# Chunked attention and a two-layer network on one core: the same work written in a new order

## The chip, the core and the metric

The kernel runs on one core of a Trainium2 chip. The metric is the time of one execution in microseconds (us) on the device, lower is better. The figure for the kernel before is the median of three runs.

## The reference

The inputs are q, k and v of 4 batches, 8 heads, 768 positions and 64 dimensions, 8 memory rows of keys and values for each batch and head, and the network's weights. Attention is computed in 24 chunks of 32 positions; each chunk sees the memory rows and its neighbourhood of 16 positions to the left and 8 to the right. The result, 3072 tokens of 512 numbers, goes through a two-layer network.

```python
scores = scale * np.matmul(q_c, k_full.transpose(0, 1, 3, 2))
a = np.exp(scores - max); a = a / sum
out[:, :, c_start:c_end] = np.matmul(a, v_full)
...
x = attn_out.transpose(0, 2, 1, 3).reshape(B * S, H * D)
h = x @ w_in                                   # 512 -> 2048
g = h + np.sin(alpha * h) ** 2 / (alpha + 1e-09)
return g @ w_out                               # 2048 -> 512
```

## The kernel before, in words

The order of all work is written out by hand as lists of two- to five-letter words, one list for a front and one for each of four passes (lines 813 to 841). `Stage.run` takes them one by one and calls the function `do_` plus the first letter; what follows is the argument. Each engine executes its own instructions in the order in which the words issue them; semaphores between engines follow from the tiles that the instructions read and write.

The front (`Stage(-1)`) computes the attention of batch 0. Pass i (0 to 3) computes the network of batch i and, in between, the attention of batch i+1, so that pass 3 has only the network.

The words that the change and the prediction speak of:

- `aNE` casts the f32 piece N of batch 0's keys (0 to 3) or queries (4 to 7) to bf16 on engine E (line 650; V is DVE, A is ACT, P is POOL). The eight pieces `kq_f` are loaded at the start by the SP queue, in the order key 0, query 0, key 1, query 1 and so on (lines 712 to 720).
- `kN`, `lN` transpose a piece on TensorE (line 269), `KNE`, `LNE` copy it out of PSUM on engine E (lines 282 and 297).
- `Vbhh` loads the values of heads h to h of batch b by two or three DMAs of the POOL queue (line 160); `dm` loads the memory values of all batches; `mN` and `H` put them among the values (lines 187 and 193).
- `IxY` loads columns of w_in, 128 for each hexadecimal digit from x up to y, in one DMA of the POOL queue (line 212); `Uxy` loads rows of w_out in the same way; `dq108` and `dk108` load all queries and keys of batch 1; `R` issues the row loads of batches 2 and 3. So `I02` brings the weights of hidden tiles 0 and 1, `I27` those of tiles 2 to 6, and `I7g` those of tiles 7 to 15.
- `s` are the scores of attention blocks with their exponentials on ACT (lines 314 and 376), `v` is the product with the values, normed on DVE (lines 339, 350 and 403), `t` (DVE) and `T` (ACT) transpose the result on TensorE and copy it into the network's input `xT` (line 362), and `c` transposes by DMA.
- `bN` and `hN` are the two halves of hidden tile N of the first layer: four matmuls each of 384 columns (line 418). `hN` also issues the sine on ACT (line 435). `qNE` squares it on engine E (line 441) and `gN` combines it into `gT` on DVE, which frees the tile's two PSUM banks (line 449). There are eight banks, hence four hidden tiles in flight.
- `fN` issues the next N matmuls of the second layer, each of 512 columns (lines 32 and 457). Where a row of output is complete, `close` copies it out on DVE or ACT and stores it by the SP queue (line 465).
- `zN` issues N matmuls on zeros, which compute nothing; `W` and `e` load an activation table and say which engines do the copies of `close`.

In the front's list the transposed attention result must be complete for the first half of the columns before `b0`, and for the second half before `h0`. In pass 0, hidden tile 7 is the eighth tile; it is the first one that needs `I7g`.

The POOL engine issues its DMAs itself, in order with its own arithmetic. At most eight of its DMAs are outstanding at a time: the DMA semaphores are taken in turn, so that the ninth waits until the first one has landed.

Of the kernel before, what the change touches and what calls it, by code (L numbers as in the profile page):

```python
# [15 lines left out]
F32 = mybir.dt.float32  # L16
ACTF = mybir.ActivationFunctionType
ALU = mybir.AluOpType


class Feed:
# [64 lines left out]
def kernel(  # L86
# [263 lines left out]
    def normed(otv, bs):  # L350
# [5 lines left out]
            in1=rinv[:].unsqueeze(3).to_broadcast([QW, 2, HP, D]),  # L356
            op=ALU.mult,
        )
# [82 lines left out]
    def squared(t, eng):  # L441
# [3 lines left out]
        else:  # L445
            e = nc.vector if eng == "V" else nc.gpsimd
            e.tensor_tensor(out=s2[:], in0=u[:], in1=u[:], op=ALU.mult)  # L447

    def finish(t, gT):
# [3 lines left out]
            in0=t["s2"][:], scalar=inv_alpha[:, ft:ft + 1], in1=t["hT"][:, :, 0:HALF],  # L453
            op0=ALU.mult, op1=ALU.add,
        )
# [275 lines left out]
    def const_b():  # L731
        for col, lo, hi in rows:
            nc.vector.tensor_reduce(
                out=biasm[:, col:col + 1], in_=ident[:, lo:hi], op=ALU.add, axis=mybir.AxisListType.X
            )
        for col in (0, 3):
            nc.vector.tensor_tensor(
                out=biasm[:, col:col + 1], in0=biasm[:, col:col + 1], in1=biasm[:, 5:6], op=ALU.add
            )
        nc.vector.tensor_scalar(  # L740
            out=biasm[:, 0:5], in0=biasm[:, 0:5], scalar1=-NEG, scalar2=NEG,
            op0=ALU.mult, op1=ALU.add
        )
# [59 lines left out]
    def const_s():  # L803
# [6 lines left out]
    first = {}  # L810
    stage = Stage(-1, None)
    stage.tile = first
    stage.run((
# [3 lines left out]
    ))  # L817
    for i, words in enumerate(((
# [6 lines left out]
    ),(  # L825
# [5 lines left out]
    ),(  # L831
# [5 lines left out]
    ),(  # L837
# [3 lines left out]
    ))):  # L841
        stage = Stage(i, stage.nx).run(words)
    feed.take(400)

# [28 lines left out]
```

## Time and profile before

| | |
|---|---|
| median of three runs | 216.53 us (216.51, 216.53, 219.29) |
| span of the profiled execution, first to last instruction | 213.1 us |
| median less span | 3.4 us |
| TensorE (PE) busy | 201.7 us, 95% of the span |
| DVE, ACT, POOL busy | 66%, 67%, 47% |
| packets of the POOL's DMA queue (q0) | 92.3% of 16 engines' span |

The profile shows one execution. Busy times are shares of the span, the chain of waits goes back from the last instruction to what released it at each step, and the table of DMA issues gives the time from issue to landing. The profiled execution's own time on the device is its span of 213.1 us and what lies around it; of the three runs, the median is 3.4 us above that span.

### The profile page before, as it was taken

The page shows a single profiled execution, that of the slowest core. Times are in us where ns is not written, and L with a number is a line of the kernel's source. Part 1 is how long each engine was busy: PE and PEld are TensorE (multiplying, and loading weights), DVE is VectorE, ACT ScalarE, POOL GpSimd, SP SyncE. Part 2 cuts the span into 40 slices and gives each one's busy share as a digit, 9 for nine tenths or more (in the row PEclk, how much of TensorE's full clock was granted, in tenths as well). Part 3 has the DMA queues.
Part 4 walks back from the last instruction along what each step waited for, and adds up shares of the span by engine and source line. Part 5 has one row for each costly group of instructions (what it writes and reads, how often), then busy time and mean ns, then how long its engine had stood idle before and what let it go on. Part 6 is the DMA issues. An engine that isn't in the chain of part 4 may idle for free.

```text
span 213.1 us, 4479 instructions
## 1 busy us (share of the span) xinstructions
PE 201.7 (95%) x1721; PEld 113.5 (53%) x1721; DVE 140.5 (66%) x218; ACT 143.5 (67%) x230; POOL 99.8 (47%) x140
## 2 busy tenths in 40 slices
PE   0799899999999999999999999999999999999994
PEld 0456555565455556555455555554555555554443
DVE  7598678999542749975856649898157197865011
ACT  2597898976857469977846199887846289891110
POOL 8959515688598193009991039659400023200000
PEclk9999999999999999999999999999999999999999
DMA  6999999999999999969999229989945400000312
GB/s 195 337 163 141 193 209 205 204 163 182 131 177 141 137 148 144 180 88 110 126 217 171 72 63 131 156 126 129 175 115 123 124 15 0 2 3 0 148 49 98
DMA packets 95908, 28.19 MB, mean 132 GB/s; under 512 B 84864, under 2 KB 92432, under 8 KB 95888
## 3 DMA queue, kind: packets, MB, share of 16 engines
q0 software_dynamic: 68736, 13.25, 92.3%
q1 hardware_dynamic: 26976, 14.62, 28.2%
q8 instruction: 13, 0.21, 0.4%
q14 instruction: 7, 0.06, 0.1%
q10 hardware_dynamic: 176, 0.04, 0.1%
HBM read 29.66 MB, written 6.29 MB: 169 GB/s over the span
## 4 chain that ended last, share of the span: by engine, by line
PE 71%; DVE 9%; DMA 7%; ACT 4%; issue 4%; POOL 3%; DVEq 0%; POOLq 0%; ACTq 0%
PE ps L462 38%; PE ps L424 27%; DMA memv_st<-in_mem_v_dram 4%; DVE gT L451 4%; DVE s L447 3%; DMA vw<-in_v_dram 3%; PE ps L414 3%; PE ps L385 2%; ACT u L439 2%; PE ps L366 1%; ACT s L444 1%; POOL s L447 1%; POOL vw L172 1%; DVE kT L285 1%; ACT L699 1%
## 5 line engine op out<-in xcount | busy, mean ns | idle before, releaser
L462 PE MATMUL ps<-w_out_sb,gT 128*128 128x512 bf16 (+2 forms) x400 | 89.1, 371 | 0.0
L424 PE MATMUL ps<-xT,w_in_sb 128*128 128x384 bf16 x512 | 86.0, 326 | 0.7 <-DVE gT L451 0.4
L451 DVE SCALAR_TENSOR_TENSOR gT<-s,inv_alpha,ps 128x768 bf16<-128x768 f32 x64 | 63.0, 1011 | 12.5 <-ACT s L444 5.2
L424 PEld LDWEIGHTS <-w_in_sb 128*128 128x128 bf16 x512 | 49.8, 98 | 35.4 <-issue 2.1
L439 ACT ACTIVATE u<-ps,alpha_sb 128x768 f32<-128x768 f32 x64 | 56.6, 895 | 16.8 <-PE ps L424 14.3
L462 PEld LDWEIGHTS <-gT 128*128 128x128 bf16 x400 | 36.6, 98 | 37.9 <-DVE gT L451 0.2
L447 POOL TENSOR_TENSOR s<-u 128x768 f32<-128x768 f32 x11 | 17.4, 1582 | 69.7 <-ACT u L439 69.7
L399 ACT ACTIVATE pt<-ps,biasm 128x256 bf16<-128x256 f32 x72 | 27.2, 489 | 10.5 <-PE ps L385 10.5
L469 DVE COPY o_sb<-ps 128x512 f32<-128x512 f32 (+1 forms) x15 | 10.1, 678 | 28.3 <-PE ps L462 26.4
L447 DVE TENSOR_TENSOR s<-u 128x768 f32<-128x768 f32 x23 | 21.9, 953 | 7.8 <-ACT u L439 7.8
L444 ACT ACTIVATE s<-u 128x768 f32<-128x768 f32 x30 | 25.0, 841 | 0.5
L354 DVE TENSOR_TENSOR x_blk<-ps,rinv 96x512 bf16<-96x512 f32 x32 | 22.0, 687 | 1.1
L469 ACT COPY o_sb<-ps 128x512 f32<-128x512 f32 (+1 forms) x10 | 5.6, 562 | 21.6 <-PE ps L462 21.6
L172 POOL DMA_DIRECT2D vw<-in_v_dram x13 | 12.9, 994 | 7.9 <-PE ps L366 5.4
L353 DVE RECIPROCAL rinv<-ps 96x8 f32<-96x8 f32 x32 | 6.4, 200 | 13.5 <-PE ps L414 12.7
L179 POOL DMA_DIRECT2D vw<-in_v_dram x13 | 12.7, 976 | 0.0
L238 POOL DMA_DIRECT2D kst<-in_k_dram x16 | 12.2, 760 | 1.1 <-DMA vw<-in_v_dram 0.8
L232 POOL DMA_DIRECT2D kst<-in_k_dram x16 | 11.3, 708 | 2.3 <-DMA vw<-in_v_dram 1.6
L369 ACT COPY xT<-ps 128x384 bf16<-128x384 bf16 x12 | 5.6, 496 | 8.2 <-PE ps L366 8.2
L245 POOL DMA_DIRECT2D q_bf<-in_q_dram x12 | 10.7, 912 | 0.0
L414 PEld LDWEIGHTS <-pt 128*128 128x128 bf16 x192 | 8.2, 97 | 4.2 <-ACT pt L399 0.3
L414 PE MATMUL ps<-vw,pt 128*128 128x65 bf16 x192 | 8.9, 193 | 0.0
(81 smaller groups left out, 131.4 us busy)
## 6 DMA issues: line engine op xcount, KB each, us to landing
out_dram<-o_sb SPq DMA_DIRECT2D x23, 256.0 KB, 2.3
kq_f<-in_k_dram SPq DMA_DIRECT2D x4, 384.0 KB, 6.5
kq_f<-in_q_dram SPq DMA_DIRECT2D x4, 384.0 KB, 6.0
q_bf<-in_q_dram POOLq DMA_DIRECT2D x12, 128.0 KB, 6.7
w_in_sb<-in_moe_w_in_dram POOLq DMA_DIRECT2D x1, 1152.0 KB, 12.6
vw<-in_v_dram POOLq DMA_DIRECT2D x7, 128.0 KB, 6.7
vw<-in_v_dram POOLq DMA_DIRECT2D x8, 112.0 KB, 7.4
kst<-in_k_dram POOLq DMA_DIRECT2D x14, 64.0 KB, 5.1
```

The lines of the kernel that those rows point to most:

```text
L172: nc.gpsimd.dma_start(vw[0:64, lo:c1, 0:D], win(vflat, a, n, 64))
L179: nc.gpsimd.dma_start(vw[72:128, c0:hi, 0:D], win(vflat, base + QW * c0 + 48, hi - c0, 56))
L354: nc.vector.tensor_tensor(out=x_blk[:].rearrange("p g e d -> p e g d"), in0=otv[0:QW, :, :, 0:D], in1=rinv[:].unsqueeze(3).to_broadcast([Q ...
L399: nc.scalar.activation(pt[:, 0:H * QW].rearrange("p (g e c) -> p g e c", g=2, e=4)[:, :, :, 32 * m:32 * m + 32], sc[:, :, 0:4 * QW].rearra ...
L414: nc.tensor.matmul(otv[:, e, hp, :], pt[:, QW * i:QW * i + P], vws[b % 2][:, 2 * hp + e, j, 0:D + 1],)
L424: nc.tensor.matmul(t["hT"][:, hf, 0:HALF], w_in_sb[:, kt, P * t["ft"]:P * t["ft"] + P], t["xT"][:, kt, HALF * hf:HALF * hf + HALF], start= ...
L439: nc.scalar.activation(t["u"][:], t["hT"][:, :, 0:HALF], ACTF.Sin, scale=alpha_sb[:, ft:ft + 1])
L444: nc.scalar.activation(s2[:], u[:], ACTF.Square)
L447: e.tensor_tensor(out=s2[:], in0=u[:], in1=u[:], op=ALU.mult)
L451: nc.vector.scalar_tensor_tensor(out=gT[:, ft, :].rearrange("p (e c) -> p e c", e=2), in0=t["s2"][:], scalar=inv_alpha[:, ft:ft + 1], in1= ...
L462: nc.tensor.matmul(o[:, c0:c1], gT[:, ft, P * s:P * s + P], w_out_sb[:, ft, c0:c1], start=(ft == 0), stop=(ft == FT - 1),)
L469: copier(state["engines"][state["o"] % len(state["engines"])])(o_sb[:, c0:c1], o[:, c0:c1])
```

## The change

Nothing is added to the work and nothing taken from it. The lists of words are replaced by new ones, named `FRONT` and `PASSES`.

- In the front, key piece 0 is cast and transposed before the alpha constants; three pieces change engines (query 0 from DVE to ACT, query 2 from DVE to POOL, and the copy `L1` from DVE to ACT); `T01` becomes `t01`. The POOL queue's order was V024, V002, V068, V046, I02, I27 and is now V024, the cast `a6P`, V002, I02, V068, V046, I27. The first product with values is `v01` where it was `v10`.
- In pass 0 the POOL queue's first loads were I7g, U69, U12, q108, k108 and are now U12, q108, I7g, U69, k108. `K1` goes from DVE to ACT, the square of tile 14 from DVE to POOL, ahead of V102, and `T3`, `T1` become `t3`, `t1`.
- In passes 1 to 3 single squares change engines (tile 13 from ACT to DVE in pass 1; tile 6 from DVE to ACT, 12 from DVE to POOL, 13 from POOL to DVE in pass 2; 6 from ACT to DVE, 14 and 15 from ACT to POOL in pass 3), some hidden tiles and attention blocks change places with their neighbours, and `V305` in pass 2 stands behind the square of tile 12 where it stood behind that of tile 13.
- Many `f` portions are split, so that copies and squares stand between them. The order of the second layer's matmuls among themselves is the same.

```diff
-        'a1A Cb Cp Cz Cv a5A eVA Cm Cl z4 a0V Ci k0 dm a4V l0 k1 K0V Ck l1 L0A V024 We L1V a2A K1A V002 '
-        'a6V k2 s00 K2V a3V s11 V068 m0 a7V s01 l2 s10 k3 K3A L2A V046 z4 v10 l3 Cs L3A I02 v11 s20 z1 '
-        'v01 s30 z1 v00 s31 z1 v30 s21 v31 T01 T10 v20 T30 T00 v21 T20 T31 I27 t11 t21 eVA Ws '
+    'a1A Cb Cm a0V k0 a4A Cl Cz a2A z4 Ci Cv l0 K0V k1 dm Ck eVA a5A V024 l1 a3V L0A K1A L1A s00 k2 Cp We '
+    'a6P V002 K2V a7V s01 s11 m0 l2 s10 k3 l3 v01 K3A L2A z4 L3A v11 z1 I02 v10 V068 s20 s30 v00 eVA s31 '
+    'v30 s21 Cs v31 T10 z1 V046 v20 z1 T30 T00 v21 T20 T31 t01 t11 Ws I27 t21 '
...
-        'o8 b0 h0 I7g q0V U69 U12 b1 h1 dq108 q1A b4 h4 b3 g0 h3 b6 g1 dk108 q4V g4 q3A b2 h2 h6 b5 h5 '
-        'Ufg g3 b7 q2V U01 U56 q6P h7 g2 q5A b10 U24 q7P g6 h10 b9 q10A g5 h9 U45 b8 h8 g7 g10 q8A q9V '
+    'o8 U12 b0 h0 q0V dq108 b1 h1 q1A b4 h4 g0 g1 I7g U69 b3 h3 dk108 b6 q4V g4 q3A b2 h2 h6 Ufg g3 b5 '
+    'q6P q2V h5 U24 b7 h7 g2 q7P q5A U56 b10 h10 g6 b9 q10A h9 g5 b8 h8 g7 g10 b11 U01 q8A q9V h11 g9 b13 '
...
-        'q15V h12 q12A b14 g15 f7 h14 V125 k1 k0 g12 l1 K1V k3 L1V L3A q14V K3A K0A V102 f9 g14 s61 f16 '
+    'g15 f2 q12A h14 f3 k1 k0 g12 l1 f1 L3A k3 f11 q14P V102 K0A L1V K1A K3A g14 f1 f1 s61 f1 f15 s70 m1 '
...
-        'b2 h2 q2V b0 h0 b4 q0A g2 h4 b3 h3 g0 o2 b1 h1 Ws q3P b6 q4V q1A h6 g4 b8 h8 g3 b5 g1 q6A h5 q5A '
+    'b2 h2 b0 q2V h0 o2 q0A b4 g2 h4 b3 h3 g0 q4V q3P Ws b1 h1 q1A b6 g4 h6 b8 g3 h8 b5 g1 h5 q6V q5A b7 '
...
```

The places of passes 1 and 2 that the prediction speaks of:

```diff
-        'h15 f7 eV We s24 q15V f6 g15 f7 V268 s05 s1 f1 m2 f14 v4 v1 f6 v0 f1 v2 f2 c4 f6 s63 s7 t1 f4 c2 '
+    'g10 f6 q11A V226 R4 b12 X8 h12 g11 q12P b14 h14 b13 V202 g12 h13 f7 q13V X6 q14A g13 b15 g14 h15 f5 '
+    's24 f4 f2 f1 q15V g15 m2 f9 V268 s05 eV s1 f14 v1 We v4 f3 f2 f1 f1 f2 v0 v2 f2 f1 f5 c2 c4 s63 f3 '
...
-        'q4A q2V h6 g2 R1 Z b7 h7 b9 h9 R1 g4 R2 q6V b8 g6 R1 eV o1 h8 q7P g7 q8A b11 h11 X1 q11A q9P b10 '
-        'g9 g8 h10 b13 g11 h13 q10V g10 b14 h14 b12 q13P X3 V305 h12 g13 q12V q14A R1 f8 eAV b15 g12 '
+    'h6 q2V g2 b7 h7 g4 Z b9 R2 eV q6A R1 h9 b8 h8 R1 q7P g6 q8A g7 q9P g9 b11 h11 q11A b10 h10 b13 h13 '
+    'g8 X1 g11 o1 q10V g10 q13V b12 h12 b14 g13 X8 X3 h14 f1 f3 R1 q14A R1 q12P f6 b15 g12 V305 f5 h15 '
```

More of the change, by code (lines that the diff above doesn't have):

```diff
@@ L18 @@
 ALU = mybir.AluOpType
+FRONT = (
[3 rows of a table added]
+)
+PASSES = ((
[6 rows of a table added]
+), (
[5 rows of a table added]
+), (
[5 rows of a table added]
+), (
[3 rows of a table added]
+))
 class Feed:
@@ L812 @@
     stage.tile = first
-    stage.run((
[3 rows of a table removed]
-    ))
-    for i, words in enumerate(((
[6 rows of a table removed]
-    ),(
[5 rows of a table removed]
-    ),(
[5 rows of a table removed]
-    ),(
[3 rows of a table removed]
-    ))):
+    stage.run(FRONT)
+    for i, words in enumerate(PASSES):
         stage = Stage(i, stage.nx).run(words)
```

23 rows, old and new, of tables (PASSES, stage) are left out of this document.

## Prediction

> **What bounds the kernel now.** I read the page first, then the busy times of five stretches (front and four passes), then the chain of waits, then TensorE's timeline at the places where the chain leaves it, and last the DMA issues.
>
> ```profile
> span 213.1 us, 4479 instructions
> ...
> PE 201.7 (95%) x1721; PEld 113.5 (53%) x1721; DVE 140.5 (66%) x218; ACT 143.5 (67%) x230; POOL 99.8 (47%) x140
> ...
> q0 software_dynamic: 68736, 13.25, 92.3%
> ```
>
> The five stretches: length, then busy time of PE, PEld, DVE, ACT and POOL.
>
> ```profile
> 0.00:24.80 24.80, 17.19 (x289) 11.45 (x290) 19.54 (x54) 15.80 (x24) 21.00 (x50) 1.00 1.82 206
> 24.80:75.50 50.70, 50.20 (x473) 28.60 (x471) 35.53 (x52) 38.24 (x63) 30.68 (x38) 1.00 1.60 174
> 75.50:122.10 46.60, 46.59 (x377) 25.73 (x374) 33.52 (x48) 32.60 (x57) 22.28 (x27) 1.00 1.56 139
> 122.10:168.10 46.00, 45.84 (x355) 24.96 (x353) 30.00 (x42) 34.04 (x57) 21.37 (x23) 1.00 1.16 122
> 168.10:213.10 45.00, 41.92 (x241) 22.80 (x239) 21.88 (x24) 22.83 (x30) 4.44 (x3) 1.00 0.13 48
> ```
>
> In the four passes PE has work nearly all the time: 50.20 of 50.70 us, 46.59 of 46.60, 45.84 of 46.00. In the last pass it is 41.92 of 45.00, and most of the rest is the store behind the last matmul. The change removes no matmul, so the passes hold under 1 us of open idle time, and a little more where matmuls are stretched by a short wait. The rest of what can move lies in the front, where PE is busy for 17.19 of 24.80 us. The chain of waits shows what holds the front up:
>
> ```profile
> 16.09 6.06 DMA vw<-in_v_dram
> ...
> 22.29 0.43 PE ps L344 x8
> ...
> 34.68 1.02 DVE gT L451
> ...
> 35.74 6.70 PE ps L424 x40
> ...
> 75.64 10.45 PE ps L424 x64
> ```
>
> The front ends on a DMA: the values of heads 4 and 5 (V046) land at 22.15, `v20` starts at 22.29, and the first hidden tile at 24.81 (next fence), 2.5 us later. From there DVE holds PE up once, at 35.74, and then matmuls follow each other to the end. 64 unbroken first-layer matmuls take 10.45 us, 0.163 us each. PE's timeline, with idle time before a group in brackets:
>
> ```profile
> 24.81 17.62 PE L424 MATMUL ps<-xT,w_in_sb 128*128 128x384 bf16 x104
> ...
> 53.52 0.51 PE L385 MATMUL ps<-qT,kT 64*128 64x96 bf16 x16 [0.20 <-DVE kT L291]
> ...
> 135.61 6.75 PE L424 MATMUL ps<-xT,w_in_sb 128*128 128x384 bf16 x40 [0.15 <-DVE gT L451]
> ...
> 180.22 9.26 PE L424 MATMUL ps<-xT,w_in_sb 128*128 128x384 bf16 x56 [0.22 <-DVE gT L451]
> ```
>
> Those are the waits that a new order could remove. The run of 104 should take 104 x 0.163 = 17.0 us and took 17.6; its first 64 matmuls should end at 24.81 + 10.45 = 35.3, and the next came at 35.74, so nearly all of that sits ahead of 35.74.
>
> **The change, part by part. First the w_in load of tiles 7 to 15 (I7g).** It moves behind U12 and all queries of batch 1 (q108) in the POOL's queue.
>
> ```profile
> w_in_sb<-in_moe_w_in_dram POOLq DMA_DIRECT2D x1, 1152.0 KB, 12.6
> q_bf<-in_q_dram POOLq DMA_DIRECT2D x1, 768.0 KB, 17.0
> k_bf<-in_k_dram POOLq DMA_DIRECT2D x1, 768.0 KB, 20.0
> w_in_sb<-in_moe_w_in_dram POOLq DMA_DIRECT2D x1, 640.0 KB, 7.9
> ...
> 18.03 2.27 POOL L213 DMA_DIRECT2D w_in_sb<-in_moe_w_in_dram  x3
> ...
> L213 POOL DMA_DIRECT2D w_in_sb<-in_moe_w_in_dram x3: 750/760/778, 18.0 to 19.5; - x3
> ...
> 21.61 0.91 POOL L155 DMA_DIRECT2D q_bf<-in_q_dram  x1
> 22.50 0.90 POOL L155 DMA_DIRECT2D k_bf<-in_k_dram  x1
> ```
>
> Issue plus time to landing: I27, the second of the three, 18.8 + 7.9 = 26.7; I7g 19.5 + 12.6 = 32.1; q108 21.6 + 17.0 = 38.6; k108 22.5 + 20.0 = 42.5. The landings come in the order of issue, and each is later than the one before by its size: 5.4 us for I7g's 1152 KB, 3.9 us for k108's 768 KB. The queue is a single file, limited by the transfer and not by its issue. So the 768 KB of q108 ahead of I7g cost 3.9 us and the 128 KB of U12 0.6 us (3.9 x 128/768): I7g lands at 36.6. Tile 7 is the eighth tile in both orders. Before, it started at 24.81 + 56 x 0.163 = 33.9, at most 0.4 later with the stretch there (I take 34.1), 2 us after its weights had landed. Now it waits for them. No cover exists: PE's order has b7 next, and the words behind it are issued behind it. ACT and DVE run dry meanwhile.
>
> **The front.** I02 moves ahead of V068 and V046, and the cast `a6P` goes into the POOL's queue between V024 and V002.
>
> ```profile
> 7.30 0.83 ACT L653 CAST k_bf<-kq_f 128x768 bf16<-128x768 f32 x1 [3.87 <-DMA kq_f<-in_k_dram]
> 8.36 0.83 ACT L653 CAST q_bf<-kq_f 128x768 bf16<-128x768 f32 x1 [0.23 <-DMA kq_f<-in_q_dram]
> ...
> 7.68 0.56 POOL L168 DMA_DIRECT2D vw<-in_v_dram  x1
> 8.21 0.89 POOL L172 DMA_DIRECT2D vw<-in_v_dram  x1
> ...
> 10.89 0.92 POOL L179 DMA_DIRECT2D vw<-in_v_dram  x1
> 14.34 1.76 POOL L172 DMA_DIRECT2D vw<-in_v_dram  x1 [2.52 <-DMA memv_st<-in_mem_v_dram]
> 16.09 0.88 POOL L179 DMA_DIRECT2D vw<-in_v_dram  x1
> ...
> 14.45 1.22 DVE L188 COPY vw<-memv_st 8x4096 bf16<-8x4096 bf16 x1
> ...
> 34.18 1.72 POOL L447 TENSOR_TENSOR s<-u 128x768 f32<-128x768 f32 x1 [6.64 <-ACT u L439]
> ...
> L760 POOL COPY mind<-asum 128x768 bf16<-128x768 bf16 x1 | 0.8, 815 | 0.0
> ```
>
> The third and fourth pieces landed at 7.3 and 8.36, 1.06 us apart; query piece 2, two pieces later, lands at 10.5. `a6P` waits for it on POOL, and eight issues wait behind it: three of V002, I02, two each of V068 and V046. The trace has no cast on POOL; it lies between the bf16 copy (0.82) and the slow square (1.72). I take 1.5, nearer the square, because it reads f32: done at 12.0. Issues at 0.89 (0.56 for V002's small one, 0.76 for I02) end at 14.3 for V002, 15.1 for I02, 16.9 for V068 and, behind two short memsets (an estimate of 1 us), 19.7 for V046. Before, its last issue ended at 17.0 and it landed at 22.15, because the file ahead was full. I take landing at 22.9, by 3 us after the last issue: 0.8 later. Its lower end is 22.15 (nothing changes); its upper end is 24.2 (the full file with I02's 256 KB ahead, 1.2 us at I7g's rate, and one issue of 1.76, as where the DVE copy stood beside it). The first hidden tile then starts at 25.6 (24.8 to 26.9). The front's other edits end earlier: ACT takes two more operations of 0.8 us, but it idled 3.87 us, and the extra 1.6 us come while PE waits for data. `K0` transposed earlier saves nothing, as V046 ends the front. `v01` now comes first and needs V002, whose last issue ends at 14.3; an idle PE there is paid only if it lasts beyond V046's landing.
>
> At 25.6 + 56 x 0.163 = 34.7 PE would reach b7, so a later front is swallowed by the wait for I7g; only a hole in the file moves I7g. I put 0.3 us for it (0 to 1.0): landing at 36.9, and the tile after b7 at 36.9 + 1.3 = 38.2 where it came at 35.74: 2.45 later. DVE, which held it up there, has caught up meanwhile.
>
> **Squares and copies on other engines, and smaller portions.**
>
> ```profile
> L447 POOL TENSOR_TENSOR s<-u 128x768 f32<-128x768 f32 x11 | 17.4, 1582 | 69.7 <-ACT u L439 69.7
> L444 ACT ACTIVATE s<-u 128x768 f32<-128x768 f32 x30 | 25.0, 841 | 0.5
> ...
> L447 DVE TENSOR_TENSOR s<-u 128x768 f32<-128x768 f32 x23 | 21.9, 953 | 7.8 <-ACT u L439 7.8
> ```
>
> Pass 0: `K1` and the square of tile 14 leave DVE (0.95 us for the square alone), which held PE up at 53.52: -0.3 us (0 to -0.4: the 0.20 and what stretched the matmul before it). The square on POOL takes 1.58 and delays V102 by about 3 us; its product `v0` comes 32 second-layer matmuls and three groups of scores later, so it is covered; its end is +0.3. `T3` and `T1` on DVE: covered. Pass 1: `v1` comes first where `v4` did and needs the last of five exponentials; I take +0.2 (0 to 0.4); the other portions and `q13V` have runs of 5 to 14 second-layer matmuls as cover: 0. Pass 2: `q6A` takes 0.95 us off DVE where PE waited 0.15 at 135.61 plus some stretch: -0.3 (0 to -0.35). `V305` and the copies of `H` wait for a square one tile (1.3 us) later, with some 30 matmuls of the second layer ahead of their first use: 0 (to +0.4). Pass 3: `q6V` no longer waits for ACT's queue: -0.15 of the 0.22 at 180.22; squares 14 and 15 on POOL end behind the last hidden tile, but 28 second-layer matmuls come before theirs: 0.
>
> Sum: 2.45 - 0.3 + 0.2 - 0.3 - 0.15 = +1.9 us on a span of 213.1, so 215.0. The median of 216.53 lies 3.4 above that span: 218.4 us.
>
> **The rivals.**
> *The weights are hidden anyway.* If I7g does not wait for q108 (the engines serve both at once, or V046 ends the front so late that PE comes at 36.6 by itself), what stays is the front's +0.8 and -0.55 from the other edits: 216.8. For it: 2 us of slack were there before. Against: four landings in single file.
>
> *Slower: POOL's issue becomes the limit.* V046's first issue took 1.76 where another took 0.89, with the DVE copy of 14.45 beside it. If each of the seven V issues behind `a6P` is stretched so, V046 and all loads behind it come 7 x 0.87 = 6.1 us later, I7g at 42 less the 1 us of hole that I counted, and the time is 218.4 + 5 = 223. It decides against 2% when five of the seven are stretched. Against it: the issues on either side of it took 0.92 and 0.88. The Trainium skill, "SBUF — State Buffer", section "SBUF: two separate sides", says that DVE and GpSimd share a port pair held for a whole instruction, so that GpSimd cannot write descriptors while DVE runs a two-port operation; the 1.76 agrees, and by that rule every DVE copy of the front is such a price.
>
> *The clock.* At the start the chip granted half speed:
>
> ```profile
> 8.74 0.85 PE L274 MATMUL ps<-ident,q_bf 128*64 128x128 bf16 x12
> ...
> 10.71 0.53 PE L274 MATMUL ps<-ident,q_bf 128*64 128x128 bf16 x12
> ```
>
> Twelve transposes took 0.85 us at 8.74 and 0.53 at 10.71. If the 2 us idle at b7 brought that back for 3 us, 3 x (1 - 0.53/0.85) = 1.1 us would be added: 219.5. No idle time in this trace after the start is long enough to show it. The Trainium skill, "TensorE: Matmul & The Clock Gate", section "HAM oscillation — how this bites in real kernels", puts the limit at idle gaps over about 3.4 us; by it the wait at b7 is too short and the sum stays.
>
> **How the numbers follow.** The wait at b7: 0.60, 218.4 us; its own range is 217.7 (I7g at 36.6, the removed waits at their full size) to 220.5 (a hole of 1.0, the ends +0.4, +0.3 and +0.4, nothing removed). Hidden: 0.25, 216.8, down to 215.8 with the front unchanged. POOL's issue: 0.09, 223. The clock: 0.04, 219.5. Something faster by over 2%: 0.02, since 4.3 us of idle time cannot be had outside a front that ends on a DMA. The range 215.8 to 220.5 holds the first, second and fourth. Two per cent, about what a measurement here tells from no change, is 212.2 and 220.9: faster 0.02, within 0.89, slower 0.09.
>
> **What would show it.** In the profile after: the landing of the 1152 KB load at 36 to 37, and an idle gap of 1.5 to 2.5 us of PE at the 57th first-layer matmul with that DMA as releaser; V046 landing at 22 to 24; no idle before the scores near 55 us; DVE no longer the releaser near 135. I am wrong if b7 starts without a wait, or if the tiles before it already come 2 us late.

## The result, and the profile after

| | before | after |
|---|---|---|
| median | 216.52 us (214.79 to 219.29, 4 runs) | 230.93 us (227.70 to 231.62, 4 runs) |
| span of the profiled execution | 213.1 us | 229.7 us |

The changed kernel is slower: 14.4 us between the medians, ratio 1.0597, 95% interval 1.0498 to 1.0696. The forecast was 218.4 us in a range of 215.8 to 220.5, with 0.09 for slower. Below, a ratio leaves out runs that are over 1.5% slower than the fastest run of the same kernel; since the changed order itself makes the clock drop, it can lie below the ratio of the medians, so both are given.

The changed kernel's profiled execution took 231.51 us, 1.8 above its span; the fourth run of before, 214.79 us, is 1.7 above the span of 213.1, so the profiled execution of before was most likely that run, the fastest of four. It has an early front: its first hidden tile came at 24.81 us, and in the profiles of the kernels below that keep its front it came between 24.64 and 26.04.

The page of the changed kernel, its first lines:

```profile
span 229.7 us, 4489 instructions
...
PE 207.4 (90%) x1721; PEld 115.4 (50%) x1721; DVE 140.9 (61%) x218; ACT 142.3 (62%) x227; POOL 105.2 (46%) x143
```

The same five stretches as before, cut where the first hidden tile of each pass starts. Columns: stretch, length, busy PE, PEld, DVE, ACT, POOL, the granted clock, DMA share, GB/s.

```profile
0.00:27.00 27.00, 17.70 (x289) 12.24 (x290) 17.52 (x52) 16.51 (x25) 20.51 (x49) 1.00 1.66 204
27.00:83.26 56.26, 52.64 (x472) 29.17 (x470) 34.79 (x53) 38.24 (x62) 33.43 (x41) 0.97 1.33 151
83.26:136.66 53.40, 48.51 (x374) 26.18 (x373) 33.99 (x48) 32.65 (x57) 22.01 (x26) 0.97 1.32 121
136.66:184.13 47.47, 46.36 (x356) 25.12 (x354) 31.24 (x42) 34.13 (x57) 20.89 (x23) 1.00 1.13 116
184.13:229.70 45.57, 42.21 (x241) 22.70 (x239) 23.39 (x25) 20.78 (x27) 8.40 (x5) 1.00 0.14 49
```

Against 24.80, 50.70, 46.60, 46.00 and 45.00 before: front +2.2, pass 0 +5.6, pass 1 +6.8, pass 2 +1.5, pass 3 +0.6, together 16.6 us of span. In passes 0 and 1 DVE, ACT and POOL are busy within 0.8 us of what they were, but for 2.8 more on POOL in pass 0, at 33.43 of 56.26: the two passes are not longer because an engine has too much to do. TensorE's timeline shows where they wait. These are its idle times of over 0.3 us from 12 us on; in brackets the idle time ahead of the group and what ended it:

```profile
18.59 0.41 PE L373 MATMUL ps<-vw,pt 128*128 128x65 bf16 x8 [1.87 <-DMA vw<-in_v_dram]
...
37.39 4.08 PE L453 MATMUL ps<-xT,w_in_sb 128*128 128x384 bf16 x24 [1.02 <-DMA w_in_sb<-in_moe_w_in_dram]
...
61.16 4.05 PE L491 MATMUL ps<-w_out_sb,gT 128*128 128x512 bf16 x12 [2.15 <-DMA w_out_sb<-in_moe_w_out_dram]
111.22 0.34 PE L414 MATMUL ps<-qT,kT 64*128 64x96 bf16 x8 [2.23 <-DMA qT<-q_bf]
114.18 0.50 PE L414 MATMUL ps<-qT,kT 64*128 64x96 bf16 x8 [2.62 <-DMA qT<-q_bf]
159.91 0.81 PE L453 MATMUL ps<-xT,w_in_sb 128*128 128x384 bf16 x4 [0.98 <-DVE gT L480]
185.32 4.87 PE L453 MATMUL ps<-xT,w_in_sb 128*128 128x384 bf16 x29 [0.37 <-DMA xT<-x_blk]
```

Six of the seven are ended by a DMA. The forecast had the second only. The large ones are the third (w_out, pass 0) and the fourth with the fifth (the transposed q, pass 1), and a stretch at half clock follows the third and the fifth. The granted clock stands before the last two columns; the first line is the time ahead of the first drop:

```profile
59.00:62.40 3.40, 1.25 (x7) 0.58 (x6) 0.61 (x1) 1.21 (x4) 2.17 (x3) 1.00 2.76 129
62.50:65.80 3.30, 3.30 (x23) 1.30 (x21) 1.22 (x1) 0.69 (x2) 3.19 (x4) 0.50 1.09 133
113.70:117.00 3.30, 2.82 (x14) 1.21 (x15) 0.00 (x0) 1.20 (x3) 2.30 (x4) 0.50 2.07 147
```

Each halved stretch lasts 3.41 us by the trace's clock records (62.45 to 65.86 and 113.65 to 117.06), so a busy TensorE loses 1.7 us in it. With the waits that makes 1.02 + 2.15 + 1.7 = 4.9 of pass 0's 5.6 us. In pass 1 the first 0.5 us of the stretch still belong to the wait, so it is 2.23 + 2.62 + (3.41 - 0.5)/2 = 6.3 of 6.8.

### The profile page after: what moved, and what is told of

Same layout as the page of the kernel before. It is cut to its first block, busy times and chain, and to the rows that moved or that the text cites. A ratio compares the mean times of both kernels' runs of the same rounds, so it can differ in the third digit from the quotient of the medians.

```text
span 229.7 us, 4489 instructions
## 1 busy us (share of the span) xinstructions
PE 207.4 (90%) x1721; PEld 115.4 (50%) x1721; DVE 140.9 (61%) x218; ACT 142.3 (62%) x227; POOL 105.2 (46%) x143
## 4 chain that ended last, share of the span: by engine, by line
PE 53%; DMA 21%; POOL 10%; DVE 5%; ACT 5%; issue 4%; SPq 1%; POOLq 0%; DVEq 0%; ACTq 0%
PE ps L491 26%; PE ps L453 22%; DMA w_in_sb<-in_moe_w_in_dram 7%; DMA memv_st<-in_mem_v_dram 4%; DMA w_out_sb<-in_moe_w_out_dram 4%; DMA vw<-in_v_dram 3%; ACT u L468 3%; DVE gT L480 3%; PE ps L443 2%; POOL s L476 2%; DMA kst<-in_k_dram 2%; DVE s L476 2%; POOL vw L201 2%; PE ps L414 2%; POOL vw L208 1%
## 5 line engine op out<-in xcount | busy, mean ns | idle before, releaser
L491 PE MATMUL ps<-w_out_sb,gT 128*128 128x512 bf16 (+2 forms) x400 | 92.4, 378 | 2.1 <-DMA w_out_sb<-in_moe_w_out_dram 2.1
L476 POOL TENSOR_TENSOR s<-u 128x768 f32<-128x768 f32 x14 | 22.2, 1589 | 88.8 <-ACT u L468 63.3
L476 DVE TENSOR_TENSOR s<-u 128x768 f32<-128x768 f32 x23 | 24.1, 1047 | 10.8 <-ACT u L468 10.8
L473 ACT ACTIVATE s<-u 128x768 f32<-128x768 f32 x27 | 22.6, 842 | 0.6
L201 POOL DMA_DIRECT2D vw<-in_v_dram x13 | 12.7, 975 | 8.0 <-PE ps L443 8.0
L208 POOL DMA_DIRECT2D vw<-in_v_dram x13 | 12.4, 956 | 2.6 <-DMA memv_st<-in_mem_v_dram 2.6
L261 POOL DMA_DIRECT2D kst<-in_k_dram x16 | 12.4, 772 | 1.8 <-DMA vw<-in_v_dram 1.8
L267 POOL DMA_DIRECT2D kst<-in_k_dram x16 | 11.7, 734 | 1.5 <-DMA vw<-in_v_dram 1.2
L414 PE MATMUL ps<-qT,kT 64*128 64x96 bf16 x192 | 7.0, 213 | 5.0 <-DMA qT<-q_bf 4.9
L414 PEld LDWEIGHTS <-kT 64*128 64x128 bf16 x192 | 5.0, 98 | 10.3 <-issue 7.5
L398 ACT COPY xT<-ps 128x384 bf16<-128x384 bf16 x9 | 4.2, 488 | 9.0 <-PE ps L395 9.0
```

The lines of the kernel that those rows point to most:

```text
L201: nc.gpsimd.dma_start(vw[0:64, lo:c1, 0:D], win(vflat, a, n, 64))
L208: nc.gpsimd.dma_start(vw[72:128, c0:hi, 0:D], win(vflat, base + QW * c0 + 48, hi - c0, 56))
L414: nc.tensor.matmul(sc[:, e, QW * hp:QW * hp + QW], kTs[b % 2][64 * e:64 * e + 64, hp, pitch * j:pitch * j + P], qTs[b % 2][64 * e:64 * e + ...
L473: nc.scalar.activation(s2[:], u[:], ACTF.Square)
L491: nc.tensor.matmul(o[:, c0:c1], gT[:, ft, P * s:P * s + P], w_out_sb[:, ft, c0:c1], start=(ft == 0), stop=(ft == FT - 1),)
```

## The experiments

Theory A: each loss has a place of its own, a DMA that was issued late or behind another. The rival: the losses come from the change as a whole (finer portions, other engines, every transfer a little later). Line numbers differ between kernels.

| kernel | median us (before, same chip) | ratio, 95% interval |
|---|---|---|
| p_front, changed front alone | 217.24 (216.13) | 1.0060 (1.0027 to 1.0092) |
| p_pass0, changed pass 0 alone | 227.31 (216.13) | 1.0411 (1.0327 to 1.0495) |
| p_pass1, changed pass 1 alone | 216.88 (216.13) | 1.0018 (0.9988 to 1.0047) |
| p_pass23, changed passes 2 and 3 | 218.17 (216.13) | 1.0111 (1.0066 to 1.0156) |
| e_i7g | 221.68 (215.80) | 1.0186 (1.0113 to 1.0260) |
| e_uef | 218.76 (215.80) | 1.0115 (1.0061 to 1.0169) |
| e_tail | 222.61 (215.80) | 1.0219 (1.0130 to 1.0308) |
| r_sq | 218.32 (215.80) | 1.0104 (1.0058 to 1.0149) |
| a_uef | 222.55 (215.84) | 1.0300 (1.0247 to 1.0353) |
| a_tail | 223.95 (215.84) | 1.0381 (1.0325 to 1.0437) |
| a_all | 219.84 (215.84) | 1.0180 (1.0127 to 1.0233) |
| best | 217.74 (215.84) | 1.0086 (1.0053 to 1.0120) |
| e_v01 | 218.71 (216.49) | 1.0115 (1.0066 to 1.0163) |
| p_front2 | 216.54 (216.49) | 1.0028 (0.9998 to 1.0058) |
| a_rest | 219.41 (216.49) | 1.0144 (1.0092 to 1.0196) |

### One part of the change at a time

```diff
-PASSES = (old 0, old 1, old 2, old 3)   FRONT = old
+p_front:  FRONT = new
+p_pass0:  PASSES = (new 0, old 1, old 2, old 3)
+p_pass1:  PASSES = (old 0, new 1, old 2, old 3)
+p_pass23: PASSES = (old 0, old 1, new 2, new 3)
```

> The changed front alone, the four passes in the order of before. Theory A (each loss has a place and a cause of its own): the first pass starts 2.2 us later, as in the changed kernel (27.00 against 24.81), and nothing of that is made up later, because TensorE limits the passes: 218.5 to 219, with no clock drop. Rival (the passes start late and lose the hold on their transfers, so that the late start sets off the later waits): over 222, with waits of TensorE in pass 0 or pass 1 that the kernel before does not have.

> The changed list of pass 0 alone. Theory A: pass 0's list holds both large losses. In it TensorE waits some 1 to 2 us at the eighth tile for the late group of w_in and some 2 us for the late group of w_out (tile 14), and the clock drops after that wait; and because its tail puts two more second-layer portions behind v5, the loads of the other half's V go out ahead of the load of mem's rows, which lands late, so that pass 1 waits for its transposed q although pass 1's own list is that of before: 226 to 230, with pass 1 longer than before by 3 us or more. Rival (pass 1's loss is of pass 1's own list): pass 1 as long as before (46.6 us), 221 to 223.

> The changed list of pass 1 alone, after pass 0 of before. Theory A: the load of mem's rows and the transposes of x start as early as before, so the transposed q is there when the scores want it: pass 1 within 1 us of before, 215.5 to 217.5. Rival (pass 1's own list makes the wait, by its loads of V issued into the time of the q transposes): pass 1 longer by 4 us or more, 220 to 224, with TensorE idle ahead of the third and fifth score tile.

> The changed lists of passes 2 and 3 alone. Theory A: in pass 2 one wait of about 1.1 us behind a square on VectorE that runs beside one on GpSimd (2.2 us for the square), the rest covered: 217 to 218.5. Rival (the waits of pass 2 in the changed kernel come from the late pass 1): no such wait, 216 to 217.

The medians lie 1.1, 11.2, 0.8 and 2.0 us above before. Their sum, 15.1, is close to the whole (14.4); the ratios add up as well, 6.0% against 5.97%. Pass 1's own list is innocent of pass 1's loss. Passes 0 and 1 of p_pass0, then pass 1 of p_pass1:

```profile
25.15:84.70 59.55, 53.22 (x466) 29.46 (x470) 34.71 (x53) 38.23 (x62) 33.03 (x41) 0.94 1.28 151
84.70:136.52 51.82, 48.03 (x367) 26.30 (x372) 33.33 (x48) 32.84 (x57) 22.30 (x26) 0.97 1.36 124
```

```profile
76.70:123.73 47.03, 46.57 (x370) 25.69 (x374) 34.14 (x48) 32.44 (x57) 22.43 (x27) 1.00 1.44 138
```

With the old list, pass 1 takes 51.82 us when the new pass 0 stands ahead of it; with the new list behind the old pass 0 it takes 47.03, where before took 46.60. Here the prediction looked for pass 1's price in the wrong list. p_pass0, p_pass1 and p_pass23 lie in their expected ranges. p_front missed its range from below: 217.24 where 218.5 to 219 was expected. Its profiled execution, 218.92 us, has a halved clock in the front; its other nine runs have a granted clock of 0.999 to 1.00.

### The three places in pass 0, put into the kernel before

```diff
 e_i7g:
-o8 b0 h0 I7g q0V U69 U12 b1 h1 dq108 q1A
+o8 b0 h0 U12 q0V dq108 b1 h1 I7g U69 q1A
 e_uef:
-h9 U45 b8 ... q13P k2 q11V Ube b15 U9b g11 Uef g13 K2V ... h14 V125
+h9 b8 ... q13P k2 U45 q11V Ube b15 U9b g11 g13 K2V ... h14 V125 Uef
 e_tail:
-T1 f3 v5 Ws T7 f8 t5
+T1 f1 v5 Ws T7 f8 t5 f2
```

> The kernel before with one edit: in pass 0 the loads U12 and q108 are issued ahead of the load of w_in's tiles 7 to 15 (I7g). Theory A: that load lands at 36.5 to 37.7 us, TensorE comes to the eighth tile at 34.1 to 34.6 and idles 2 to 3 us for it, and the clock is halved for one or two windows of 3.4 us, which adds up to 1.7 us each: 218.5 to 222. Rival (the wait alone, without the clock): 218 to 219 and a granted clock of 1.00. Rival (the late landing is made by other words of pass 0's list): lands before 34, 216 to 217.

> The kernel before with three words moved in pass 0: U45 behind the square of tile 13 on GpSimd, and V125 ahead of the load of w_out's tile 14 (Uef). Theory A (the wait for Uef at 59 us in the changed kernel is the price of its place in the queue): Uef is issued 3 us later and lands at 58 to 61, where it is needed at 55, with 1 to 3 us idle of TensorE there and a clock drop if the wait fills over half of a window: 218 to 221. Rival (it was late only because the whole file was late behind the first loads): it lands before its use, 216 to 217.

> The kernel before with two of pass 0's last second-layer matmuls moved from ahead of v5 to the end of the pass. Theory A (the transposes of x in pass 1 start late since the load of mem's rows finds the loads of V, issued 0.4 us earlier beside it, ahead of it): the load of mem's rows takes 5 to 7 us where it took 4.1, the transposes start 1 to 3 us later, and TensorE waits up to 3 us at the scores of pass 1: 217 to 221. Rival (0.4 us at that place does not matter, and pass 1's wait comes from the late file of pass 0 as a whole): the load takes about 4 us and pass 1 as long as before, 216 to 217.

**e_i7g**: +5.9 us. TensorE waits for the weights at the eighth tile, and the clock is halved for 6.83 us (38.45 to 45.28 in the clock records, from 0.8 us ahead of the wait's end on):

```profile
39.27 7.01 PE L452 MATMUL ps<-xT,w_in_sb 128*128 128x384 bf16 x24 [3.06 <-DMA w_in_sb<-in_moe_w_in_dram]
```

```profile
38.50:45.20 6.70, 5.93 (x19) 2.85 (x20) 1.62 (x3) 2.22 (x3) 2.16 (x3) 0.50 1.23 196
```

The 24 matmuls take 7.01 us; the same 24 took 4.08 in the changed kernel at 37.39. The load landed at 39.22, later than the 36.9 of the prediction, in an execution whose file ran late already (1.30 us idle for the load I27, at 29.54). 3.06 us of wait and half of the 6.0 us of halved clock behind it make 6.1, and its pass 0 is 57.75 us long, 7.1 more than before.

**e_uef**: +3.0 us, but not where Theory A had put it:

```profile
51.76 0.81 PE L490 MATMUL ps<-w_out_sb,gT 128*128 128x512 bf16 x3 [1.75 <-DMA w_out_sb<-in_moe_w_out_dram]
...
59.12 1.24 PE L490 MATMUL ps<-w_out_sb,gT 128*128 128x512 bf16 x5 [0.22 <-DMA w_out_sb<-in_moe_w_out_dram]
```

In the old order of the second layer U45 is needed first, and its later issue is paid at once; after that wait tile 14 costs 0.22 us. So both places cost; which one is paid depends on the portions around. A part of the 3.0 us belongs to neither: in the profiled execution TensorE also waits for the keys of batch 1, a load issued ahead of all that was moved, where the kernel before had no wait.

```profile
45.27 0.53 PE L302 MATMUL ps<-ident,k_bf 128*64 128x128 bf16 x12 [0.85 <-DMA k_bf<-in_k_dram]
```

For the changed kernel a_uef below decides.

**e_tail**: two matmuls, 0.4 us of work, change place, and the kernel is 6.8 us slower in the median (3.3 to 7.7 in its four runs). The POOL's loads V226 (two DMAs) and the SP's load of mem's rows in the kernel before, in the changed one and in e_tail:

```profile
75.94 1.12 POOL L172 DMA_DIRECT2D vw<-in_v_dram  x1
76.54 0.91 SPq L253 DMA_DIRECT2D kst<-memv_st  x1
77.03 1.16 POOL L179 DMA_DIRECT2D vw<-in_v_dram  x1
80.76 10.73 SPq L260 DMA_TRANSPOSE kT<-kst  x8
```

```profile
83.25 1.11 POOL L201 DMA_DIRECT2D vw<-in_v_dram  x1
84.35 1.15 POOL L208 DMA_DIRECT2D vw<-in_v_dram  x1
84.50 0.91 SPq L282 DMA_DIRECT2D kst<-memv_st  x1
91.83 11.44 SPq L289 DMA_TRANSPOSE kT<-kst  x8
```

```profile
76.93 1.12 POOL L200 DMA_DIRECT2D vw<-in_v_dram  x1
78.02 1.16 POOL L207 DMA_DIRECT2D vw<-in_v_dram  x1
78.49 0.91 SPq L281 DMA_DIRECT2D kst<-memv_st  x1
86.14 11.31 SPq L288 DMA_TRANSPOSE kT<-kst  x8
```

V226 stands in POOL's queue behind V378, which overwrites values that `v5` needs, the last product of pass 0; the SP's load stands behind the last stores of the pass. Matmuls moved from ahead of `v5` to the end of the pass bring V226 earlier against the SP's load. Before, it is issued between V226's two DMAs and the transposes start 4.2 us behind it; in the other two it is issued behind both, and they start 7.3 and 7.6 us behind it. In e_tail this is the 3.4 us by which the transposes are late, and the scores of pass 1 pay:

```profile
105.55 0.34 PE L413 MATMUL ps<-qT,kT 64*128 64x96 bf16 x8 [1.92 <-DMA qT<-q_bf]
108.13 0.50 PE L413 MATMUL ps<-qT,kT 64*128 64x96 bf16 x8 [2.23 <-DMA qT<-q_bf]
```

with 6.83 us of half clock, which starts during the second wait (106.34 to 113.17 in the clock records). All 17 traces agree: in the 13 kernels where the SP's load is issued ahead of V226's second DMA, the transposes start 4.1 to 4.7 us behind it; in the four where it is issued behind that DMA (the changed kernel, p_pass0, e_tail and a_uef), 6.5 to 7.6. That the place of the two matmuls does it is shown; that the SP's packets then wait behind V226's in the DMA engines is argued from these issue times, for no run moved the SP's load itself.

### The same three places, put back in the changed kernel

```diff
 a_uef:
-V158 g8 l0 q13P l2 l3 U45 L0A ... U9b V125 b15 h15 g13 Uef K2V
+U45 V158 g8 l0 q13P l2 l3 L0A ... U9b Uef V125 b15 h15 g13 K2V
 a_tail:
-t1 f2 v5 Ws f3 f1 T7 f4 t5 f2
+t1 f4 v5 Ws f3 f1 T7 f4 t5
 a_all: both, and
-o8 U12 b0 h0 q0V dq108 b1 h1 q1A b4 h4 g0 g1 I7g U69 b3
+o8 b0 h0 I7g q0V U69 U12 b1 h1 dq108 q1A b4 h4 g0 g1 b3
```

> The changed kernel with U45 ahead of V158 and with the load of w_out's tile 14 (Uef) ahead of V125 in pass 0. Theory A (the 2.1 us idle at 59 us and the halved clock behind it are the price of these two places): that load lands before 57, no wait and no clock drop near 60, pass 0 shorter by 3 to 4 us, pass 1 as long as in the changed kernel: 226.5 to 228.5. Rival (the file of loads is late as a whole behind the first loads, so that another load is late instead): a wait of over 1 us stays between 50 and 65 us, 229.5 to 231.5.

> The changed kernel with two of pass 0's last second-layer matmuls put back ahead of v5. Theory A (their place sets whether the load of mem's rows goes out ahead of the V loads): that load takes about 4 us, the transposes of x start 2 to 3 us earlier against the pass's start, the waits at the scores of pass 1 (4.9 us with the halved clock 1.7 more) vanish or shrink below 1 us: 224 to 226.5. Rival (pass 1 is late through the whole of pass 0): pass 1 stays over 50 us, 229 to 231.5.

> The changed kernel with three orders put back in pass 0: the load of w_in's tiles 7 to 15 ahead of U12 and q108, the two places of the run before last (U45, Uef), and the two matmuls ahead of v5. Front, all squares and copies on other engines, the split portions and passes 1 to 3 stay as changed. Theory A (these few places in queues hold nearly all of the loss, and the front and passes 2 and 3 the rest, 1 and 2 us): 218 to 220.5, no wait over 1.2 us, no clock drop. Rival (the splitting and the other engines cost by themselves): 222 or more.

**a_uef**: the wait and the halved clock near 60 us are gone, and pass 0 is 52.75 us long where it was 56.26, as expected. The median fell by 8.4 us, more than expected: the profiled execution (227.08 us) still has a halved clock in pass 1, but three of the four runs have a granted clock of 1.00 and took 222.12 to 222.56. Its waits at the scores, 1.58 and 1.85 us, are shorter than the 2.23 and 2.62 of the changed kernel and near the edge of what halves the clock. Pass 1 is still 52.32 us long in that profile: the SP's load is issued 0.12 us behind V226's second DMA.

**a_tail**: 223.95, just below the expected 224 to 226.5; pass 1 takes 46.98 us and has no wait. The SP's load is issued between V226's two DMAs again.

**a_all**: 219.84, inside the expected range; the granted clock of its four runs is 0.998 to 1.00. Passes 0 and 1:

```profile
26.51:77.65 51.14, 50.72 (x472) 28.77 (x470) 34.63 (x52) 38.37 (x62) 32.25 (x40) 1.00 1.63 168
77.65:124.64 46.99, 46.96 (x377) 25.72 (x375) 34.16 (x48) 32.44 (x57) 22.43 (x27) 1.00 1.46 138
```

51.14 and 46.99 where before had 50.70 and 46.60. With these few places put back, all in pass 0, the kernel is 4.0 us above before where the change was 14.4. The finer portions and the other engines, which all stay, are not the large loss.

### The front

```diff
 e_v01, on the kernel before:
-z4 v10 l3 Cs L3A I02 v11 s20 z1 v01 s30
+z4 v01 l3 Cs L3A I02 v11 s20 z1 v10 s30
 p_front2, on p_front:
-l3 v01 K3A L2A z4 L3A v11 z1 I02 v10 V068 s20
+l3 v10 K3A L2A z4 L3A v11 z1 I02 v01 V068 s20
```

> The kernel before with v01 and v10 exchanged in the front, so that the first product with values is the one that needs the load V002, as in the change. Theory A (the front's 1.1 to 1.3 us are paid where TensorE waits for V002, since the scores, exponentials and products that follow it are one chain to the end of the front): TensorE idles until that load lands near 18 us, the scores behind it start 1 to 2 us later, and the first hidden tile comes 0.8 to 2 us later: 216.8 to 217.8. Rival (the prediction's step: idle there is paid only if it lasts beyond the landing of V046): no change, 215.8 to 216.2.

> The changed front alone, with v10 and v01 exchanged, so that the first product needs V024 as before. Theory A: the front's loss of 1.1 to 1.3 us shrinks to 0.5 or less: 216 to 216.7. Rival (the loss comes from the places of the V loads and I02, or from the other order of casts): 217 to 217.5.

e_v01 is 2.2 us slower, 0.9 above the top of its expected range, and in it TensorE stands where V002 has not landed:

```profile
18.50 0.41 PE L372 MATMUL ps<-vw,pt 128*128 128x65 bf16 x8 [2.75 <-DMA vw<-in_v_dram]
```

A part of this is the clock: five of the six runs have a granted clock of 0.992 or less, and in the profiled one it is halved from 19.16 to 22.57, right behind this wait, and once more in pass 2. The one run at a clock of 1.00 took 217.81, 1.3 above before.

p_front2, where `v10` is first again, is at 216.54 against 216.49. By the medians the front's loss is gone; by the ratios 0.3% is left of p_front's 0.6%, and the two intervals overlap. Its profile has the first hidden tile at 27.01, no earlier than the new front has it without the exchange (26.51 to 27.19, but for p_front's 29.00 with the halved clock). How much of the front's loss lies in this exchange stays open. V046 holds TensorE up until 22.66 in it (its landing was forecast at 22.9):

```profile
17.24 0.41 PE L372 MATMUL ps<-vw,pt 128*128 128x65 bf16 x8 [0.62 <-DVE vw L216]
...
22.66 0.41 PE L372 MATMUL ps<-vw,pt 128*128 128x65 bf16 x8 [1.54 <-DMA vw<-in_v_dram]
```

### Passes 2 and 3, and two more versions

```diff
 r_sq, on p_pass23 (pass 2):
-q13V
+q13A
 best, on the kernel before:
-K1V k3 L1V L3A q14V K3A    pass 2: q6V    pass 3: q6A
+K1A k3 L1V L3A q14P K3A    pass 2: q6A    pass 3: q6V
 a_rest = a_all with the old FRONT and q13A in pass 2
```

> The lists of passes 2 and 3 of the change in the kernel before, with one more edit: in pass 2 the square of tile 13 goes to ScalarE where the change has it on VectorE beside a square on GpSimd. Theory A (the square of 2.26 us on VectorE is so slow because of the other beside it, and it alone holds TensorE for about 1 us): no wait of TensorE ahead of tile 14 or 15, and the time is 1 us below that of the two lists as changed: 216.5 to 217.3. Rival (the wait is of the order of tiles and transposes of pass 2): the wait stays at about 1 us, 218.

> The kernel before with only those moves between engines that take VectorE off the path: in pass 0 K1 on ScalarE and the square of tile 14 on GpSimd, in pass 2 the square of tile 6 on ScalarE, in pass 3 the square of tile 6 on VectorE. Theory (the four short waits behind VectorE, 0.15 to 0.36 us each, vanish): 0.5 to 0.8 us below the kernel before, 215 to 215.6. Rival (each moves the wait to the next instruction): within 0.2 us of the kernel before.

> The changed kernel with the three orders of pass 0 put back, the front of before, and the square of tile 13 in pass 2 on ScalarE. Theory A (the losses are separate and add): 1.1 us less for the front and up to 0.7 less for pass 2 than with the three orders alone (219.84): 218 to 218.8, still 2 above the kernel before, of which 0.4 lie in pass 1 and the rest in passes 2 and 3. Rival (the split portions and other squares gain once the waits are gone): 216 or less.

The stall in pass 2 of p_pass23: a square on VectorE beside one on GpSimd.

```profile
142.50 1.46 POOL L475 TENSOR_TENSOR s<-u 128x768 f32<-128x768 f32 x1 [3.34 <-ACT u L467]
142.52 2.26 DVE L475 TENSOR_TENSOR s<-u 128x768 f32<-128x768 f32 x1
...
145.95 0.81 PE L452 MATMUL ps<-xT,w_in_sb 128*128 128x384 bf16 x4 [0.97 <-DVE gT L479]
```

VectorE's square takes 2.26 us where its mean before was 0.95. With it on ScalarE (r_sq) the wait is gone and pass 2 takes 46.41 us where it took 47.48, as Theory A had it. But the medians of r_sq and p_pass23 are 218.32 and 218.17, on chips whose kernel before stood at 215.80 and 216.13: the stall is explained, the time is not moved by it as far as these runs can tell. Pass 3 waits 0.30 to 0.37 us for the last transposed block in both. r_sq is still 2.5 us above before. In its profile passes 2 and 3 are 0.3 and 1.5 us longer, 0.9 of that behind the last matmul, and its runs lie 2.1 us above their spans where those of before lie 1.7 to 1.8; that is 2.1 of the 2.5 us. What lengthens the end stays open.

**best** is 1.9 us slower than before, where 0.5 to 0.8 faster was expected. Its pass 2:

```profile
135.81 0.83 ACT L472 ACTIVATE s<-u 128x768 f32<-128x768 f32 x1
...
137.74 1.46 PE L452 MATMUL ps<-xT,w_in_sb 128*128 128x384 bf16 x8 [1.52 <-DVE gT L479]
```

The square of tile 6 was taken from VectorE to end a wait of 0.15 us. ScalarE came to it behind a sine of a later tile (135.01 to 135.91); the combination waited for the square, TensorE for the combination, 1.52 us. A second wait, 0.51 us, appeared in pass 0 behind ScalarE's copies.

**a_rest** missed its 218 to 218.8. Pass 2 gains (46.35 us where a_all had 47.46) and the front starts pass 0 at 24.64 instead of 26.51, but pass 0 gives 1.4 back (52.53 against 51.14), 0.99 us for a load of w_out and 0.52, at 44.07, for the keys:

```profile
55.05 0.38 PE L491 MATMUL ps<-w_out_sb,gT 128*128 128x512 bf16 x1 [0.99 <-DMA w_out_sb<-in_moe_w_out_dram]
```

The file of loads lands when it lands (this w_out load at 55.01, in a_all at 55.10), so a front that ends earlier meets it earlier. The losses of front and pass 0 do not simply add. No version here beats the kernel before.

## Why the prediction was wrong, point by point

The step that failed is the sum behind `b7`. It gave the rest of pass 0 "-0.3", pass 1 "+0.2", and took the clock as whole. The profile has 4.6 us more in the rest of pass 0 and 6.8 in pass 1: a w_out load that had come to stand behind others in POOL's queue (2.15 us), the SP's load of mem's rows issued behind V226 (4.85 us at the scores), and a halved clock behind each. The wait for I7g, the largest term of the sum, came where it was forecast and was the small one.

**The load of w_in's tiles 7 to 15: right in mechanism and place.** It landed at 37.34 in the changed kernel (forecast 36.9), with the releaser as forecast. The wait was 1.02 us where 1.5 to 2.5 was forecast, because the front was 2.2 late and not 0.8; in p_pass0, with the old front, it was 3.06.

**The clock: its chance of 0.04 was too low.** The prediction gave the halved clock 1.1 us, once, after b7 alone. In the changed kernel it came twice, for 1.7 and about 1.5 us, though not at b7, where the wait was 1.02; in e_i7g and p_pass0 it came for 6.83 us at that very wait, 3.06 us long. The Trainium skill's limit of about 3.4 us, "TensorE: Matmul & The Clock Gate", section "HAM oscillation — how this bites in real kernels", was quoted there as a reason for no drop; the rows disagree: 2.15 us of idle time was enough at 61.16, 3.06 in e_i7g. The measurement decides; the last section works out an edge from the traces.

**Pass 0's queue was priced for its first loads only.** The prediction's sum had, behind b7, only "-0.3" for pass 0. It did not look at where the later loads U45, V125 and Uef stand against each other and against the square of tile 13 on GpSimd. POOL's timeline, before and then after:

```profile
43.45 1.82 POOL L447 TENSOR_TENSOR s<-u 128x768 f32<-128x768 f32 x1 [2.81 <-ACT u L439]
45.22 2.12 POOL L219 DMA_DIRECT2D w_out_sb<-in_moe_w_out_dram  x3
```

```profile
46.72 1.81 POOL L476 TENSOR_TENSOR s<-u 128x768 f32<-128x768 f32 x1 [2.27 <-ACT u L468]
48.48 2.10 POOL L248 DMA_DIRECT2D w_out_sb<-in_moe_w_out_dram  x3
50.56 1.00 POOL L201 DMA_DIRECT2D vw<-in_v_dram  x1
51.52 1.03 POOL L208 DMA_DIRECT2D vw<-in_v_dram  x1
52.51 0.63 POOL L248 DMA_DIRECT2D w_out_sb<-in_moe_w_out_dram  x1
```

Before, Uef is the last of the three issues that start at 45.22, at 46.77. After, the square is 3.27 later (the 2.2 of the front and the 1.0 of the wait for I7g), U45 stands behind it (0.6), and the two DMAs of V125 ahead of Uef (2.0): issued at 52.51, landed at 61.12, and needed at 59.02. a_uef shows it: 3.5 us of pass 0 and the halved clock go with these two places. The prediction followed POOL's file load by load for I7g, and not here.

**Pass 1: "0" and "+0.2" were the largest error; it became 6.8 us longer.** Its list was judged by cover inside pass 1. The cause stands at the end of pass 0, in a change of two matmuls that were thought free because TensorE's own order of work does not care; SP's queue and POOL's queue do. a_tail and e_tail show it from both sides.

**The front: +0.8 was near p_front's +1.1, by luck.** V046 landed about as late as forecast in p_front2 (22.66), but in the changed kernel the wait ahead of 22.65 ends on ScalarE and is 0.16 us. The step "an idle PE there is paid only if it lasts beyond V046's landing" failed: e_v01 does nothing else and costs 2.2 us, 1.3 in the run without a drop of the clock. That scores, exponentials and products behind that place form the chain to the end of the front is the likely reason. Also, the cast `a6P` does not run on POOL as the prediction and the list of words said: the code sends every letter but A to VectorE, so query 2 did not change its engine. V002's issues start at 7.56 us after and at 7.68 before; the POOL issues were not held, and no run shows the price of a cast there.

**Squares: "-0.3" for q6A in pass 2 and "0" for the squares that went elsewhere failed in pass 2.** In the changed order q13V met q12P and cost 0.97 us. The Trainium skill, "SBUF — State Buffer", section "SBUF: two separate sides", cited in the prediction for issues beside copies, also says that of a VectorE operation with two inputs in SBUF and a GpSimd operation that reads SBUF one waits for the whole of the other; 2.26 us, not far below 1.46 + 0.95, agrees. In the old order, best shows, the move itself turns into a wait of 1.52 us.

**Pass 3: "-0.15" became +0.6.** VectorE's wait is gone, but TensorE waits 0.37 us for the last transposed block at 185.32; what makes the rest stays open.

**POOL's stretched issue came once, not five times.** In the changed kernel V046's first issue stands beside the copy of the memory values, as it did before:

```profile
16.12 1.51 DVE L217 COPY vw<-memv_st 8x4096 bf16<-8x4096 bf16 x1
...
16.50 1.57 POOL L201 DMA_DIRECT2D vw<-in_v_dram  x1
```

The front's other issues of V loads took 0.70 to 0.90 us. Nor is every copy on VectorE such a price, as the prediction had it: before, the issues at 9.08 and 9.96 took 0.90 and 0.94 us with VectorE's copies of 8.99 to 10.46 beside them.

**The chances.** 0.09 for slower came from one rival, a stretched issue on POOL. Each loss that came was of a kind the prediction knew (a load behind another), but it had counted one such place where three had been moved, and took the half clock as unlikely though its own wait of 2 us was the condition. The upper end has a slip too: the terms named for 220.5 add up to 220.8.

## What to carry to other kernels

When a list of work is reordered, go through each DMA queue, not only TensorE's list: for every load, write down what stands ahead of it now that did not before, the engine work that its issuing engine must wait for included, and the time at which it is first needed. A load that another queue issues beside it counts too: 0.4 us of TensorE's work, moved past a wait of POOL, changed which of two loads was issued first, and that was worth 6.8 us here. And price waits of TensorE that add up to about 1.8 us or more within 3.4 us with the half-speed stretch behind them.

## What the runs showed of the hardware

- **The clock.** In every trace with clock records, the stretches at whole and at half clock that lie between two changes are multiples of 3.413 us (after: 47.787 is 14 of them, 3.413 one). Counted on that grid, TensorE stood idle for 1.81 to 3.07 us of the 3.41 us ahead of each of the eleven drops inside the kernels (2.12 and 3.07 in the changed kernel, 1.81 in a_tail, 1.84 in p_front and e_v01), and for 1.64 us at most in a stretch after which the clock stayed whole (p_pass0, 60.69 to 64.10). So the edge lies between 1.64 and 1.81 us in one such stretch here, and where a wait falls decides: 2.00 us in a_uef at 18.79 lay 1.48 and 0.52 us on the two sides of a border, and the clock stayed whole; 2.04 us in p_front at 19.11 lay 1.82 us on one side, and it was halved. No run was made to move a wait against this grid.
- **A small load beside a large one.** The 64 KB load of mem's rows let the transposes start 4.1 to 4.7 us after its issue when one DMA of V226 was issued ahead of it (13 kernels), and 6.5 to 7.6 us when two were (four kernels).
- **VectorE beside GpSimd.** One square of 128x768 took 2.26 us with a square on GpSimd from the same moment, where the mean of the 23 before is 0.95. An issue of a V load by GpSimd took 1.76 us (before) and 1.57 (after) beside VectorE's copy of the memory values, 0.88 and 0.86 right behind it.
